# Two groups instead of one by seven block products in an attention and mixer kernel, with every engine's order written out

## The chip, the cores and the metric

The kernel runs on one core of one Trainium2 chip. The core has five engines with instruction queues of their own that run in order: TensorE (PE, matrix products into PSUM), VectorE (DVE), ScalarE (ACT), GpSimd (POOL) and SyncE (SP, which here only issues DMAs). Semaphores tie them together. The metric is the device time in microseconds (us), the median of several runs. Before the change it is 247.61 us (three runs, 247.29 to 248.21).

## The reference

```python
# linear attention, batch 8, heads 8, sequence 576, head size 64
phi(x) = np.where(x > 0, x, np.exp(x) - 1.0) + 1.0
kv  = einsum('bhsd,bhse->bhde', phi(k), v)      # per head
num = phi(q) @ kv;  den = phi(q) @ sum(phi(k)) + 1e-6
x   = num / den                              # to [8, 576, 512]
# mixer
h   = maximum(x.T @ w_tok1, 0) @ w_tok2      # along the sequence, 576 -> 256 -> 576
u   = x + h.T
h2  = maximum(u @ w_ch1, 0) @ w_ch2          # along channels, 512 -> 1536 -> 512
out = u + h2                                 # fp32
```

The kernel computes in bf16 with fp32 sums.

## The kernel before

The eight batches follow one another. A batch's 576 positions are four tiles of 128 and a tail of 64; the tails of two batches are handled together. For each batch the steps are:

- loads of q, k and v (576 KB each half) by SP into one buffer per tensor for batches 2 to 7 (`load`, L132);
- phi: an exponential on ACT (`phi_exp`, L151), add and max on DVE (`phi_add`, L157), a minimum on DVE (`phi_end`, L165); a cast of v (`vcast`, L176);
- `kv` (L191) on PE with copies on ACT (L197); phi(q) is transposed by a DMA (`qtr_dma`, L221); `nd_all` (L261) gives numerators and denominators on PE, and DVE divides (L270 to L289);
- `mm1` (L312) and `mm2` (L325), the token mixing, and the residual add on DVE (L337) that gives u; u is transposed by a DMA (`utr_dma`, L521) into uT, which the next step reads;
- the first channel mixing, `mm3` (L543): twelve chunks of 128 of the 1536 channels, each 4 matmuls of 512 columns, read by a Relu on ACT (L550) into cr;
- the second channel mixing by a seven-product block scheme (Strassen's, in Winograd's form): `row_sums` (L655) make sums of blocks of cr on DVE, `pair_product` (L852) makes seven products, `pair_copy` (L857, ACT) and `pair_end` (L861, DVE, and L863, POOL) put them together with u, and `pair_put` (L867) sends the batch out by POOL's queue.

In batches 2 to 6 four of the twelve chunks (4, 5, 10 and 11) do not go through `mm3` but also through seven block products (`mix_one`, L712). A group g takes chunks 2g and 2g+1 of the first half of the channels and the same chunks of the second half. Products 1 to 7 are 4 matmuls of 256 columns each. Their right sides are blocks of uT and four sums of such blocks (`u_sums`, L689, into tuc); their left sides are blocks of the weights and four sums of these (`group_sums`, L700, into swc), made once. Products 1, 6 and 5 are copied from PSUM by ACT (L720), product 4 is read by a Relu on ACT (L718), and products 2, 3 and 7 by a DVE operation that adds the copy and takes the Relu (`add_relu`, L531). Products 1, 6, 7 and 4 accumulate on one PSUM bank one after the other, with a read between them; 5 and 3 do so on another. Batch 7 does this for all three groups (`mix_first`, L740) and its second mixing without pairs (`product`, L768, `product_read`, L778).

The order of the work is the order of the calls, since the kernel is under a manual schedule. Each stage of batches 0 to 6 is a list `big` of PE's steps and a list `fill` of (position, step) that are put between them; batch 7 follows a string, `SEQUENCE`. A PSUM bank comes from a ring or from small tables beside each function. Output tiles come from eight slots that are taken in turn (`o_slots`), four a batch.

Of the kernel before, what the change touches and what calls it, by code (L numbers as in the profile page):

```python
# [15 lines left out]
EPS = 1e-6  # L16


@with_exitstack
def kernel(  # L20
# [43 lines left out]
    ring = {1: 0, 2: 0}  # L64

    def bank(at=None):
        if at is None:
            at, ring[1] = ring[1], (ring[1] + 1) % 4
        return psum[:, at]

    def banks(at=None):
        if at is None:
            at, ring[2] = 4 + ring[2], (ring[2] + 2) % 4
        return psum[:, at:at + 2]

    def two16():
        return banks().bitcast(BF16).rearrange("p a (t s) -> p a t s", s=128)
# [24 lines left out]
    uTj = [t.rearrange("p r j c -> p (r j c)").rearrange("p (j r c) -> p j r c", j=NDM, r=R) for t in uT]  # L102
    uTt = const("uTt", [128, 2, NDM, 128])
    cr = [const(f"cr{b}", [128, NCH, SM]) for b in range(2)]
    crt = const("crt", [128, NCH, 128])
    obuf = const("obuf", [128, 8, DM], FP32)
    swc = const("swc", [128, 4, 2, 256])
# [31 lines left out]

    live = {}  # L140
    o_at = [0]

    def o_slots(m):
        at = o_at[0] if o_at[0] + m <= 8 else 0
        o_at[0] = (at + m) % 8
        return obuf[:, at:at + m]

    def phi_exp(nm, n, j0, nj):
        f = raw[nm, rb(n)][:, j0:j0 + nj].rearrange("p j f -> p (j f)")
        e = work.tile([128, 2 * TD], BF16, name="e", tag="e", bufs=4)[:, :nj * TD]  # L150
        nc.scalar.activation(out=e, in_=f, func=AF.Exp)  # L151
        live["e", nm, n, j0] = e

    def phi_add(nm, n, j0, nj):
        f = raw[nm, rb(n)][:, j0:j0 + nj].rearrange("p j f -> p (j f)")
        y = work.tile([128, 2 * TD], BF16, name="y", tag="y")[:, :nj * TD]
        nc.vector.tensor_scalar(out=y, in0=f, scalar1=1.0, scalar2=1.0, op0=ALU.add, op1=ALU.max)  # L157
        for j in range(nj):
            live["y", j0 + j] = y[:, j * TD:]

    def phi_end(nm, n, j0, nj):
        c, i = divmod(j0, 2)
        dst = (kp if nm == "k" else qp)[:, c, :, i:i + nj]
        e, y = live["e", nm, n, j0], live["y", j0][:, :nj * TD]
        live["phi"] = nc.vector.tensor_tensor(  # L165
            out=dst.transpose([0, 2, 1, 3]), in0=e.rearrange("p (i t d) -> p i t d", i=nj, t=T),
            in1=y.rearrange("p (i t d) -> p i t d", i=nj, t=T), op=ALU.min)

    def phi(nm, n, c):
        phi_exp(nm, n, 2 * c, 2)  # L170
        phi_add(nm, n, 2 * c, 2)
        phi_end(nm, n, 2 * c, 2)

    def vcast(n, c, copy=nc.scalar.copy):
        js = slice(2 * c, 2 * c + 2)
        copy(out=vs[:, js, :, 0:D],  # L176
             in_=raw["v", rb(n)][:, js].rearrange("p j (t d) -> p j t d", t=T))

    def bank16():
        return bank().bitcast(BF16).rearrange("p (t s) -> p t s", s=128)  # L180
# [3 lines left out]
    def kv(n, cs):  # L184
        b = n % 2
        ps = banks(4 if n > 1 else None)[:, :, 0:2 * D1].rearrange(
            "p a (c e) -> p a c e", c=2)
        for c in cs:
            for t in range(T):
                for a, i in QUARTERS:  # L190
                    nc.tensor.matmul(out=ps[half[i], a, c], lhsT=kp[half[a], c, t, i],  # L191
                                     rhs=vs[half[a], 2 * c + i, t],
                                     start=(t == 0), stop=(t == T - 1))
        cs = slice(cs[0], cs[-1] + 1)
        for i in range(2):
            at = slice(i * D1, (i + 1) * D1)
            nc.scalar.copy(out=kvbd[b][half[i], cs, :, at].transpose([0, 2, 1, 3]),  # L197
                           in_=ps[half[i], :, cs])
# [6 lines left out]
    TS = [range(0, 5), range(5, T)]  # L205

    def qtr_put(n, c, ts, tp, put, dst=None):
        v_ = (qT[n % 2] if dst is None else dst)[:, 0:4 * TD].rearrange("p (a c t s) -> p a c t s", a=2, c=2, t=T)
        put(out=v_[:, :, c, ts[0]:ts[-1] + 1].transpose([0, 2, 1, 3]),
            in_=tp[:, 0:len(ts)].rearrange("p t (a s) -> p t a s", a=2))  # L210

    def qtr(n, c, put=nc.scalar.copy):
        tp = two16()
        for h, ts in enumerate(TS):
            qtr_mm(c, ts, tp[:, h])
        for h, ts in enumerate(TS):
            qtr_put(n, c, ts, tp[:, h], put)

    def qtr_dma(n, halves=range(2)):
        for a in halves:  # L220
            live["crossbar"] = nc.sync.dma_start_transpose(  # L221
                out=qT[n % 2][:, 2 * TD * a:2 * TD * (a + 1)].rearrange("p (f s) -> p f s", s=D),
                in_=qp[half[a]].rearrange("p c t i d -> p (c t i d)"))

    def nd_mm(n, c, rs):
        b = n % 2
        ps = banks()
        for s_, r in enumerate(rs):
# [5 lines left out]
        live["nd", c, rs[0]] = ps  # L234

    def nd_end(n, g, rs):
        b = n % 2
        m = len(rs)
        v_ = live["nd", g, rs[0]][:, 0:m, 0:HG * D1].rearrange("p r (h e) -> p r h e", h=HG)
# [9 lines left out]

    def nd_all(n):
        b = n % 2
        ps = [psum[:, 2 + 2 * m:4 + 2 * m] for m in range(3)]
# [10 lines left out]
        xv = x[b].rearrange("p r (c i a d) -> p i (r c) a d", c=2, i=2, a=2)  # L265
        v_ = [ps[m][:, :, 0:D1 * 7].rearrange("p i (k e) -> p i k e", k=7) for m in range(3)]
        dens = work.tile([128, 2, 2, 7], FP32, name="dens", tag="dens", bufs=1)
        last = work.tile([128, 2, 6], FP32, name="dens2", tag="dens2", bufs=1)
        both = psum[:, 2:6, 0:D1 * 7].rearrange("p b (k e) -> p b k e", k=7)
# [4 lines left out]
        def six(m, k0, rc0):  # L274
            den = (dens[:, m] if m < 2 else last)[:, :, k0:k0 + 6]
            nc.vector.tensor_tensor(  # L276
                out=xv[:, :, rc0:rc0 + 3],
                in0=v_[m][:, :, k0:k0 + 6, 0:D].rearrange("p i (q a) d -> p i q a d", a=2),
                in1=den.rearrange("p i (q a) -> p i q a", a=2)[
                    :, :, :, :, None].to_broadcast([128, 2, 3, 2, D]), op=ALU.mult)  # L280

        for m, at in enumerate((6, 0)):
            six(m, m, 4 * m)
            nc.vector.tensor_tensor(
                out=xv[:, :, 3, m], in0=v_[m][:, :, at, 0:D],
                in1=dens[:, m, :, at, None].to_broadcast([128, 2, D]), op=ALU.mult)
        nc.vector.tensor_scalar(out=last, in0=v_[2][:, :, 0:6, D], scalar1=EPS, scalar2=None,
                                op0=ALU.add)
        nc.vector.reciprocal(out=last, in_=last)  # L289
        six(2, 0, 7)  # L290

    def nd(n, g, rs):
        nd_mm(n, g, rs)
        nd_end(n, g, rs)
# [1016 lines left out]
```

## Time and profile before

| | |
|---|---|
| median of three runs | 247.61 us |
| span of the profiled execution | 246.4 us, 1.2 below the median |
| PE busy | 236.1 us (96%) |
| DVE busy | 198.8 us (81%) |
| ACT busy | 139.3 us (57%) |
| POOL busy | 76.9 us (31%) |
| DMA | 48.40 MB, mean 196 GB/s |
| L543, the chunks with 512 columns | 252 records, 60.2 us |
| L712, the products of the one group in five batches | 140 matmuls of 256 columns, 20.2 us |

Busy time is a union of an engine's instructions, with the parts in which a matmul drains while the next runs; so PE's 96% does not say by itself how full its stream is. A group's line gives the number of its instructions and, after the bar, busy time and mean length of one in ns, then the engine's idle time before them and what ended it. In a timeline each row is a start, a length, the engine, the line, and the tiles written and read.

### The profile page before, as it was taken

Reading aid. Unit: us, or ns where it says so; the run is one execution under the profiler, and the core shown is the slowest. Engines: PE = TensorE matmul, PEld = TensorE weight load, DVE = VectorE, ACT = ScalarE, POOL = GpSimd, SP = SyncE. Lnnn points to the kernel's source line nnn. Section 1 sums busy time; section 2 is a strip of 40 time slices with the busy share of each in tenths; the row PEclk is TensorE's granted clock in tenths of the full one; section 3 lists DMA queues with packets and bytes.
Section 4 is the critical chain, followed back from the end, with each engine's and each line's share of the span. In section 5 each row is a group of like instructions: output and inputs, shape, how many; then the busy total and the mean of one; then the engine's idle time right before and its main releaser. Section 6 shows DMA issues by size and latency. Waiting matters only on the chain.

```text
span 246.4 us, 6090 instructions
## 1 busy us (share of the span) xinstructions
PE 236.1 (96%) x2477; PEld 162.3 (66%) x2496; DVE 198.8 (81%) x349; ACT 139.3 (57%) x224; POOL 76.9 (31%) x88
## 2 busy tenths in 40 slices
PE   7789999999999899999999999999999999999993
PEld 3475455564868456865678556865676567888883
DVE  5955877889799998988894499979996779956973
ACT  4673881569774367736897167656852652175100
POOL 9670030296703600061004500071007700440360
PEclk9999999999999999999999999999999999999999
DMA  6999999999726796589979955459748702352055
GB/s 248 267 203 258 348 275 308 355 251 289 294 24 133 223 334 271 132 224 210 358 263 174 412 148 192 93 115 329 228 89 94 170 3 43 64 112 61 4 127 130
DMA packets 50444, 48.40 MB, mean 196 GB/s; under 512 B 30192, under 2 KB 36720, under 8 KB 50416
## 3 DMA queue, kind: packets, MB, share of 16 engines
q1 hardware_dynamic: 41984, 35.00, 48.2%
q0 software_dynamic: 7472, 12.22, 22.7%
q10 hardware_dynamic: 960, 0.79, 1.4%
q8 instruction: 19, 0.31, 0.5%
q14 instruction: 9, 0.07, 0.1%
HBM read 35.85 MB, written 9.44 MB: 184 GB/s over the span
## 4 chain that ended last, share of the span: by engine, by line
PE 84%; DVE 6%; DMA 5%; issue 3%; ACT 1%; SPq 0%; DVEq 0%
PE ps L543 22%; PE ps L852 18%; PE ps L712 6%; PE ps L312 6%; PE ps L583 5%; PE ps L740 4%; PE ps L768 4%; PE ps L325 4%; DMA q_raw<-in_q_dram 3%; PE ps L557 2%; PE ps L570 2%; DMA uT<-u 2%; PE ps L820 2%; PE ps L261 2%; PE ps L191 1%
## 5 line engine op out<-in xcount | busy, mean ns | idle before, releaser
L543 PE MATMUL ps<-uT,wc 128*128 128x512 bf16 x252 | 60.2, 379 | 0.8 <-DMA uT<-u 0.5
L550 ACT ACTIVATE cr<-ps 128x512 bf16<-128x512 f32 x59 | 34.7, 600 | 32.9 <-PE ps L543 32.7
L543 PEld LDWEIGHTS <-wc 128*128 128x128 bf16 x256 | 24.1, 98 | 25.1 <-DMA uT<-u 0.8
L863 POOL TENSOR_TENSOR obuf<-obuf,q_raw 128x512 f32<-128x512 f32 x6 | 8.1, 1344 | 93.3 <-DVE obuf L861 59.1
L852 PE MATMUL ps<-k_raw,v_raw 128*128 128x256 bf16 x216 | 24.9, 273 | 0.0
L852 PEld LDWEIGHTS <-v_raw 128*128 128x128 bf16 x216 | 21.0, 98 | 3.9 <-issue 0.4
L852 PEld LDWEIGHTS <-cr 128*128 128x128 bf16 x216 | 21.1, 98 | 3.7
L861 DVE TENSOR_TENSOR obuf<-ps,u 128x512 f32<-128x512 f32 x24 | 16.3, 685 | 8.1 <-PE ps L852 5.8
L151 ACT ACTIVATE e<-q_raw 128x1152 bf16<-128x1152 f32 x16 | 18.3, 1163 | 7.3 <-DVE x L244 5.5
L151 ACT ACTIVATE e<-k_raw 128x1152 bf16<-128x1152 f32 x16 | 18.2, 1165 | 2.7 <-DMA k_raw<-in_k_dram 2.7
L852 PE MATMUL ps<-wc,cr 128*128 128x256 bf16 x144 | 17.7, 273 | 0.0
L276 DVE TENSOR_TENSOR x<-ps,dens 128x768 bf16<-128x768 f32 x18 | 17.2, 953 | 0.4
L655 DVE TENSOR_TENSOR v_raw<-cr 128x768 bf16<-128x768 bf16 (+2 forms) x24 | 14.8, 617 | 2.1 <-ACT cr L718 2.1
L337 DVE TENSOR_TENSOR u<-ps,x 128x1024 bf16<-128x1024 f32 x12 | 14.6, 1217 | 0.4 <-PE ps L325 0.3
L176 ACT CAST vs<-v_raw 128x1152 bf16<-128x1152 f32 x12 | 13.5, 1161 | 0.0
L312 PE MATMUL ps<-x,w 128*128 128x512 bf16 x49 | 13.0, 379 | 0.3
L165 DVE TENSOR_TENSOR qp<-e,y 128x1152 bf16<-128x1152 bf16 x16 | 11.9, 753 | 1.6 <-ACT e L151 0.9
L165 DVE TENSOR_TENSOR kp<-e,y 128x1152 bf16<-128x1152 bf16 x16 | 12.7, 816 | 0.5 <-ACT e L151 0.4
L157 DVE TENSOR_SCALAR y<-k_raw 128x1152 bf16<-128x1152 f32 x16 | 11.7, 763 | 1.3 <-DMA k_raw<-in_k_dram 1.3
L157 DVE TENSOR_SCALAR y<-q_raw 128x1152 bf16<-128x1152 f32 x16 | 12.4, 793 | 0.4 <-DMA q_raw<-in_q_dram 0.4
L325 PE MATMUL ps<-ar,w2p 128*128 128x512 bf16 x44 | 11.8, 379 | 0.3
L583 PE MATMUL ps<-wc,cr 128*128 128x512 bf16 x47 | 11.9, 379 | 0.1
(182 smaller groups left out, 458.8 us busy)
## 6 DMA issues: line engine op xcount, KB each, us to landing
k_raw<-in_k_dram SPq DMA_DIRECT2D x16, 576.0 KB, 7.6
q_raw<-in_q_dram SPq DMA_DIRECT2D x16, 576.0 KB, 5.9
v_raw<-in_v_dram SPq DMA_DIRECT2D x14, 576.0 KB, 9.2
out_dram<-obuf POOLq DMA_DIRECT2D x12, 512.0 KB, 6.9
wc<-in_moe_w_ch_dram POOLq DMA_DIRECT2D x8, 384.0 KB, 9.8
out_dram<-obuf POOLq DMA_DIRECT2D x4, 256.0 KB, 6.0
out_dram<-obuf ACTq DMA_DIRECT2D x12, 64.0 KB, 2.2
out_dram<-obuf SPq DMA_DIRECT2D x12, 64.0 KB, 1.9
```

What stands on the lines that cost most here:

```text
L151: nc.scalar.activation(out=e, in_=f, func=AF.Exp)
L157: nc.vector.tensor_scalar(out=y, in0=f, scalar1=1.0, scalar2=1.0, op0=ALU.add, op1=ALU.max)
L165: live["phi"] = nc.vector.tensor_tensor(out=dst.transpose([0, 2, 1, 3]), in0=e.rearrange("p (i t d) -> p i t d", i=nj, t=T), in1=y.rearran ...
L276: nc.vector.tensor_tensor(out=xv[:, :, rc0:rc0 + 3], in0=v_[m][:, :, k0:k0 + 6, 0:D].rearrange("p i (q a) d -> p i q a d", a=2), in1=den.r ...
L312: nc.tensor.matmul(out=ps[:, mt], lhsT=w1t[:, b, ms] if r == R else w1[:, r, ms], rhs=x[b][:, r, :], start=(r == 0), stop=(r == R))
L325: nc.tensor.matmul(out=ps[:, i], lhsT=w2v(kt, r, b), rhs=ar[b][:, kt, :], start=(kt == 0), stop=(kt == NT - 1 and not add))
L543: nc.tensor.matmul(out=ps, lhsT=wc1[:, kj, 128 * mc:128 * mc + 128], rhs=uTj[b][:, kj] if n < 2 else uT[b][:, :, kj], start=(kj == 0), sto ...
L550: nc.scalar.activation(out=cr[b][:, mc, :], in_=ps, func=AF.Relu)
L583: nc.tensor.matmul(out=ps, lhsT=crt[:, kc, :] if t == 8 else cr[b][:, kc, 128 * r:128 * r + 128], rhs=wc2[:, kc, :], start=(kc == 0), stop ...
L655: return engine.tensor_tensor(out=s_[which - 1][:, ks], in0=x_, in1=y_, op=op)
L852: nc.tensor.matmul(out=live[tile_][:, j], lhsT=lhs[:, k_], rhs=rhs[:, k_], start=(first and j == 0 and k_ == 0), stop=(k_ == KH - 1), skip ...
L861: nc.vector.tensor_tensor(out=o, in0=live[tile_], in1=u[n % 2][:, d::2, HC[c]], op=ALU.add)
```

## The change

- Group 1 (chunks 2, 3, 8 and 9) of batches 2 to 6 goes through the seven block products as well. `mix_one` becomes `mix_mm` and `mix_read` with the group as an argument, swc holds the weight sums of both groups, and group 1's three copies lie in the spaces of the third and fourth row sums (`HOLD`).
- obuf has six output slots instead of eight; the batches 1 to 6 all use slots 0 to 3.
- Every step is split into a part for each engine, and each part has a name, such as `4x12` (batch 4, group 1, product 2 on PE) or `4y12` (its read). One string, `ORDER`, lists all names from batch 0 to 7, and the program is emitted in that order. The PSUM bank of each step is in a table, `BANK`, the buffers of the exponentials and of y in `EBUF` and `YBUF`, the output slots in `SLOT`. `GATE` names the four loads that wait for another transfer.
- In the program, matmuls of 512 columns go from 466 to 386 and those of 256 from 961 to 1101; DVE has 19 instructions more, 15 that add and take the Relu and 4 weight sums; ACT and POOL have as many as before, and so have the DMAs.

```diff
+NO = 6
+GSW = {2: 0, 1: 1}
+HOLD = {2: 'p0 p1 p2', 1: 's2 s3 s2'}
+GATE = {'1k0': ('wc1', 0), '2q0': ('wc2', 1), '4q0': ('u', 2, 1), '7q0': ('u', 5, 1)}
...
+BANK = {k_: int(v_) for k_, v_ in (e.split(":") for e in """2K:5 2n0:2 2n1:4 2n2:6 2f:2 2g0:5 2g1:2 2X2:7 2Z2:0 2Y2:2 2gt:6 3K:6 3n0:2 3n1:4 3n2:6 3f:3 3g0:2 3g1:4 3X2:1
...
+SLOT = {k_: int(v_) for k_, v_ in (e.split(":") for e in """0o0:0 0o1:2 1P:0 V0:4 2P:0 3P:0 V1:4 4P:0 5P:0 6P:0 7P0:4 7t:0 7P1:2""".split())}
...
+ORDER = """A2 A0 A1 A3 A4 A5 A6 A8 A9 A7 A10 A12 A13 A14 A11 A16 A17 A15 A19 A18 A21 A20 A22 A23 A24 A25 A26 A27 A28 A29
...
+2m7 5Lq1 2r1 W0 2s1 4kx0 4qb1 2x21 2x11 2s2 1o 3n1 2x22 2y21 2x25 2r7 2y22 2x26 2y25 2x15 2s3 2y11 2x12 2s4
+2y26 2x23 2y12 2r0 2x16 4qa0 4qx0 2x27 3f0 2y23 2y15 2y27 2y16 2p10 4qb0 3fr0 2x13 4v0 2w10 2x17 4qT0 2y13 3f1
...
-    ring = {1: 0, 2: 0}
-
-    def bank(at=None):
-        if at is None:
-            at, ring[1] = ring[1], (ring[1] + 1) % 4
-        return psum[:, at]
+    def bank(name):
+        return psum[:, BANK[name]]
...
-    obuf = const("obuf", [128, 8, DM], FP32)
-    swc = const("swc", [128, 4, 2, 256])
+    obuf = const("obuf", [128, NO, DM], FP32)
+    swc = const("swc", [128, len(GSW), 4, 2, 256])
...
-    def group_sums():
-        a11, a12, a21, a22 = [cblock(m, h)[:, :, 512:768] for m in range(2) for h in range(2)]
...
+    def group_sums(g, which):
+        s_ = swc[:, GSW[g]]
+        a11, a12, a21, a22 = [cblock(m, h)[:, :, 256 * g:256 * g + 256] for m in range(2) for h in range(2)]
...
+    def mix_read(n, g, i):
+        ps = mix_tile(n, g, i)
+        if n == B - 1:
+            c1, c6, c5 = hold[g]
+        else:
+            c1, c6, c5 = [hold_at[w[0]][int(w[1])] for w in HOLD[g].split()]
+        dst = lambda m, e: cr[n % 2][:, KH * m + 2 * g:KH * m + 2 * g + 2, HALF[e]]
+        if i == 4:
+            nc.scalar.activation(out=dst(1, 0), in_=ps, func=AF.Relu)
+        elif i in (1, 6, 5):
+            nc.scalar.copy(out={1: c1, 6: c6, 5: c5}[i], in_=ps)
+        else:
+            o, c = {2: (dst(0, 0), c1), 3: (dst(0, 1), c6), 7: (dst(1, 1), c5)}[i]
+            add_relu(o, ps, c)
...
+    for n in range(2, B):
+        for g in range(3) if n == B - 1 else GSW:
+            for i in range(1, 8):
+                put(f"{n}x{g}{i}", mix_mm, n, g, i)
+                put(f"{n}y{g}{i}", mix_read, n, g, i)
...
+    for name in ORDER.split():
+        tok[name]()
```

In the names, the first digit is the batch. `m` is a chunk of 512 columns and `r` its read, `x` and `y` a block product of the first mixing and its read, `s` a sum of blocks of uT, `G` a sum of weight blocks, `w` a row sum, `p` a product of the second mixing, `c`, `e`, `h` its copies, its adds on DVE and its adds on POOL, `o` the output DMAs, `n` the normalisation, `f` and `g` the token mixing, `K` the key-value product, `uT` and `qT` the transposing DMAs, `L` a load, and `T`, `U`, `V`, `W` a tail.

## The prediction

> **What bounds the kernel now.** I read the page's first part, then the chain, the waits of TensorE (PE), the timelines around the two places where PE stood still, and the busy time by stretch.
>
> ```profile
> PE 236.1 (96%) x2477; PEld 162.3 (66%) x2496; DVE 198.8 (81%) x349; ACT 139.3 (57%) x224; POOL 76.9 (31%) x88
> ...
> PE 84%; DVE 6%; DMA 5%; issue 3%; ACT 1%; SPq 0%; DVEq 0%
> ```
>
> PE is busy 96% of the span and 84% of the chain that ended last, so what is taken from PE's stream can show in the time. A busy PE need not be a full one, so next come starts. In the chain, stretches of one shape give the pace:
>
> ```profile
> 53.30 7.34 PE ps L543 x34
> ...
> 156.49 3.93 PE ps L852 x36
> ```
>
> A 512-column matmul takes 7.34/34 = 0.216 us from start to start, a 256-column one 3.93/36 = 0.109 us. Between 21 and 242 us nearly every pair of matmuls keeps this pace. Two gaps do not:
>
> ```profile
> 82.98 1.90 PE L543 MATMUL ps<-uT,wc 128*128 128x512 bf16 x8
> 85.50 0.80 PE L261 MATMUL ps<-kvbd,qT 64*128 64x65 bf16 x40 [0.62 <-DVE obuf L610]
> ...
> 187.64 1.47 PE L852 MATMUL ps<-q_raw,cr 128*128 128x256 bf16 x12
> 189.61 1.68 PE L543 MATMUL ps<-uT,wc 128*128 128x512 bf16 x7 [0.50 <-DMA uT<-u]
> ```
>
> Eight matmuls of 0.216 us from 82.98 on reach 84.71, and the next starts at 85.50: 0.79 us lost, for a bank that VectorE (DVE) had not read. Twelve of 0.109 from 187.64 on reach 188.95, and the next starts at 189.61: 0.66 us lost, for a transposing DMA. Together 1.4 us of stall; the rest is PE's own work.
>
> ```profile
> 63.00:84.00 21.00, 20.89 (x244) 15.29 (x244) 20.37 (x31) 12.08 (x17) 7.67 (x7) 1.00 0.51 138
> 84.00:109.20 25.20, 24.48 (x274) 16.88 (x274) 23.35 (x41) 16.55 (x25) 4.91 (x7) 1.00 0.78 241
> ...
> 139.20:164.40 25.20, 25.10 (x277) 17.15 (x278) 22.73 (x38) 16.47 (x25) 3.97 (x5) 1.00 0.59 170
> ```
>
> The columns are length, PE, PEld, DVE, ACT, POOL busy, then PE's granted clock (1.00 throughout). The reader is to see DVE's column: 20.4 of 21.0, 23.4 of 25.2 and 22.7 of 25.2 us. DVE is the second bound, and the change gives it work.
>
> **The PE term.** In batches 2 to 6 four chunks of the first channel mixing, each 4 matmuls of 512 columns, become seven products of 4 matmuls of 256. Per batch 16 x 0.216 = 3.46 us go, 28 x 0.109 = 3.05 us come: -0.40 us, over five batches -2.0 us. The other matmuls are the same in number and shape, only moved. All of it lies on PE's stream, so it counts in full if nothing else becomes late.
> [...] The rows above say 0.109 and 0.216, a half, and the measurement decides.
>
> **The ACT term: zero.** Four Relu reads (L550, 600 ns) become three copies (L720, 579 to 588 ns) and one Relu (L718, 591 ns) per batch. ACT is busy 16.5 of 25.2 us in the stretch above. What hides it is PE's stream; with that cover gone it would cost nothing more, being no longer.
>
> **The DVE term.**
>
> ```profile
> L531 DVE CUSTOM_DVE_ANT_0 cr<-ps,part 128x512 bf16<-128x512 f32 x6 | 4.1, 688 | 2.5 <-PE ps L740 1.6 <-ACT part L720 0.8
> L276 DVE TENSOR_TENSOR x<-ps,dens 128x768 bf16<-128x768 f32 x18 | 17.2, 953 | 0.4
> ```
>
> Per batch three add-and-Relu reads are new (L531, 0.69 us long, 0.61 apart back to back): +1.8 us. Once, four sums of weight blocks for the second group (L700, 0.42 us undisturbed): +1.4 to 1.7 us. Together +10.8 us on an engine that is busy 198.8. The batch from 139.2 goes from 22.7 to 24.5 us of DVE work while its PE work goes from 25.2 to 24.8; the one from 84.0 goes from 23.4 to 25.1, more than its PE work of 25.2 - 0.8 - 0.4 = 24.0, unless work moves to a neighbour. So the redrawn order decides. I added up DVE's and PE's new queues between the same marks, with durations of the batch from 139.2 (normalisation with L276 4.1 us a batch, phi 8 x 0.67, row sums 3.9, residual adds 2 x 1.14, output adds 4 x 0.61). From the normalisation products of batch 2 to those of batch 4 it has 42.0 us of DVE work against 44.2 of PE (95%), from 4 to 5 29.2 against 33.3 (88%), from 5 to 7 40.8 against 43.7 (93%). It fits everywhere, because batches 4 and 5 now start their first chunks before the last products of the batch in front, and some of phi and of the weight sums stands earlier. Following batches 2 and 3 read by read with PE at full pace, DVE is ready ahead of each consumer by little: 0.2 us for batch 2's last product of group 1, 0.3 for product 6 of its second mixing, 0.4 for product 3, 0.35 for batch 3's product 7 of group 2.
> Every new wait stands in such a chain: a product with its copy and the next product on the same bank. Behind a late DVE read stand the other DVE reads in its queue, and for them PE's next product. Each late read costs PE what exceeds its margin. From below: 0, since all margins are positive, and no gain beyond the removed gaps; from above, DVE's idle time of 2.5 us in the batch from 139.2 (25.2 - 22.7) stays as it is, which gives a batch of 24.5 + 2.5 = 27.0 us. I take +0.6 us over the five batches, nearest to the lower end, since the margins are positive in every stretch I followed and the tightest load is 95%.
>
> **The moved steps.** The gap at 84.71 goes: between the tail's last product and batch 3's normalisation, which needs its bank, now stand 2.1 us of other PE work for the tail's reader (L610 before). So does the one at 188.95: batch 6's last residual add is ready some 5.8 us of PE work ahead of its first consumer, and that transfer took 5.2 us at its longest (median 3.1 us). -1.4 us for both; what is late next is batch 7's first transfer, with about 4.6 us of PE work ahead of its consumer, between those two figures, bound 0 to +0.6 us, taken at 0 (the median). On SP the transposes now stand between loads, and only two loads still wait for a transpose; the tail's transpose of batch 3 stands behind three loads, where that transfer took 8.1 us in the median, with 9 us of PE work ahead of its reader: 0, and up to +2 if the loads are slower.
> POOL issues the same work. Its adds hold up DVE where DVE's operands are all in SBUF:
>
> ```profile
> 78.91 2.49 DVE L165 TENSOR_TENSOR kp<-e,y 128x1152 bf16<-128x1152 bf16 x2
> 81.32 1.27 DVE L861 TENSOR_TENSOR obuf<-ps,u 128x512 f32<-128x512 f32 x2
> 82.52 1.11 DVE L700 TENSOR_TENSOR swc<-wc 128x512 bf16<-128x512 bf16 x1
> ...
> 79.07 1.71 POOL L863 TENSOR_TENSOR obuf<-obuf,q_raw 128x512 f32<-128x512 f32 x1 [0.59 <-DVE obuf L861]
> 82.08 1.27 POOL L863 TENSOR_TENSOR obuf<-obuf,w 128x512 f32<-128x512 f32 x1 [1.29 <-DVE obuf L861]
> ```
>
> The two phi ends should take 1.42 us and took 2.49; the weight sum took 1.11 for 0.42. The PSUM read between them kept its 0.68. In the new order POOL's adds and its weight sums stand beside normalisation reads, which come from PSUM, so I count nothing; where an SBUF operation falls beside one, the price is up to 1.1 us of DVE.
> [...]
> Six output slots for eight: every batch now writes the same four. A batch's first output add comes 15 us of PE work or more after the DMA of the one before is issued, and that DMA lands in 6.9 us: hidden; with the cover gone, up to 7 us once.
> The prologue to 21 us and the 3.8 us behind the last matmul keep their instructions: 0.
>
> **Sum.** 246.4 - 2.0 - 1.4 + 0.6 = 243.6 us of span. The runs' median of 247.6 lies 1.2 above the profiled span, for what lies around it: 244.8 us.
>
> **Rivals.**
> A: DVE becomes the bound, slower. For it: 95% of load in the first two mixed batches, and in-order reads each of which waits for PE or ACT. Against: the margins above. Its place is batches 2 to 6; it decides from the point where DVE's idle time per batch exceeds 25.2 - 24.5 = 0.7 us. With half of today's 2.5 us the batch is 25.75, +0.55 x 5 = +2.8, less the removed gaps: 247.6 - 1.4 + 2.8 = 249.0. With all of it, +1.8 x 5: up to 255.
> B: the order hides nothing more than before: the stream gets shorter, but new small waits eat it (0.5 us a batch, one lost margin each, 2.5 in all): 247.6 - 2.0 - 1.4 + 2.5 = 246.7, no change.
> C: a transpose is late behind loads at one or two places: +2 to +4, 247 to 249.
> D: PE's stream gets no shorter: that needs 3.46 / 28 = 0.123 us for a 256-column matmul, and all such groups show 0.109; 246.8.
>
> **How the numbers follow.** Saturated stream 0.70 (243.2 to 246.3); B 0.12; A 0.12 (half of it below 250); C 0.06, half each side of 248.8. Low end: no new wait, and another 1 us of small gaps of 0.1 to 0.3 us gone too: 244.8 - 0.6 - 1.0 = 243.2. High end 249.2, A at half its idle time. The saturated case alone spans 243.2 to 246.3. A measurement here tells about 0.5% from no change, 1.2 us. Faster 0.71, same 0.14, slower 0.15.
>
> **What would show it.** Right: 80 matmuls of 512 columns fewer and 140 of 256 more at 0.216 and 0.109 us; DVE about 209 us busy, over 90% from 63 us on, PE's waits still under 2 us between 21 and 240. Wrong: PE waits for DVE's L531 counterparts or for banks, several times 0.3 us in each of batches 2 to 6 (A, B); PE waits for a transpose (C); DVE operations of over 1 us beside POOL's adds.

## The result

The changed kernel takes 248.70 us (median of 15 runs, 247.87 to 249.53), the kernel before 247.35 us (15 runs beside them): ratio 1.0043, 95% interval 1.0030 to 1.0056. Forecast were 244.8 us and a gain; it is a loss of 1.35 us, small (0.4%) but with an interval that leaves out no change. In short: PE's stream did get shorter, by half of what was forecast, and the last stores to DRAM came late by more than that.

The kernel before was profiled once more as a control: span 245.9 us, time 247.72. In the 15 runs of the changed kernel time minus span is 1.73 to 1.87 us, in the control 1.8. So the profile that the prediction was read from (span 246.4) belongs to a run of 248.2 us, one of the slower ones, and not to the median.

The profile after, its first part and its chain:

```profile
PE 235.1 (95%) x2538; PEld 168.5 (68%) x2556; DVE 204.1 (83%) x368; ACT 136.9 (56%) x224; POOL 78.7 (32%) x88
...
PE 88%; DVE 3%; DMA 3%; issue 2%; ACT 2%; DVEq 0%; SPq 0%; ACTq 0%
```

PE is busy 1.0 us less than in the first profile, DVE 5.3 us more; PE's share of the chain is 88% where it was 84%. These shares don't show the loss. I cut both traces at three marks: the start of the first channel-mixing matmul, the start of the last matmul, the end of DVE's last output add.

| us | control | changed | forecast of the change |
|---|---|---|---|
| up to the first channel-mixing matmul | 20.54 | 20.43 | 0 |
| from there to the last matmul | 221.35 | 219.87 (-1.48) | -2.8 |
| last matmul to the end of the last add | 0.74 | 0.73 | 0 |
| end of the last add to the end of the span | 3.32 | 5.53 (+2.21) | 0 |
| span | 245.9 | 246.6 | -2.8 |

PE wins half of what was forecast, and the stretch behind the last add eats more than that. One profile stands on each side. PE's stretch in the second row is 221.34 to 221.36 us in three of four profiles of the kernel before and 219.3 to 220.2 us in nine of ten of the changed kernel (runs with another store order or warm-up, told below, counted in), so that its gain is known to some 0.5 us. PE's timeline in the changed kernel has three places where a pair of rows does not close up:

```profile
33.09 1.03 PE L736 MATMUL ps<-wc,cr 128*128 128x512 bf16 x4
34.61 1.17 PE L309 MATMUL ps<-identity,qp 128*128 128x128 bf16 x18 [0.50 <-ACT cr L684]
...
141.58 1.05 PE L917 MATMUL ps<-uT,wc 128*128 128x256 bf16 x8
142.91 0.60 PE L917 MATMUL ps<-crt,swc 128*128 128x256 bf16 x4 [0.28 <-ACT q_raw L932]
...
162.99 1.47 PE L959 MATMUL ps<-wc,q_raw 128*128 128x256 bf16 x12
164.72 0.79 PE L376 MATMUL ps<-kvbd,qT 64*128 64x65 bf16 x40 [0.26 <-DMA qT<-qp]
```

Four matmuls of 0.216 us from 33.09 end their turn at 33.95, and the next starts at 34.61: 0.66 us, for ACT's read of a bank. Eight of 0.109 from 141.58 reach 142.45: 0.46 us, for a copy on ACT. Twelve from 162.99 reach 164.30: 0.42 us, for a transposing DMA. None of them is DVE's. The same stretches as in the prediction (84.0 and 139.2) show how full DVE is now:

```profile
84.00:109.20 25.20, 25.09 (x326) 18.50 (x321) 24.35 (x43) 16.04 (x25) 7.39 (x9) 1.00 0.75 218
...
139.20:164.40 25.20, 24.87 (x293) 18.47 (x292) 22.92 (x39) 15.29 (x24) 5.01 (x6) 1.00 0.71 180
```

24.35 of 25.2 us in the first, and PE's column beside it says 25.09: DVE is busy 97% of it, and the profile lists no wait of PE for DVE between 21 and 241 us.

The end of both kernels, in timelines of DVE, SP and ACT. The last batch's output goes out in 24 stores of 64 KB, one half of each quarter tile by SP and one by ACT. The control:

```profile
242.20 0.42 DVE L778 TENSOR_TENSOR obuf<-ps,u 128x256 f32<-128x256 f32 x1 [0.25 <-PE ps L768]
...
241.36 1.76 SPq L798 DMA_DIRECT2D out_dram<-obuf  x3
```

The last add ends at 242.62, and SP's last three issues are over at 243.1: the last stores go out when their adds end. The changed kernel:

```profile
240.61 0.42 DVE L1019 TENSOR_TENSOR obuf<-ps,ut 128x256 f32<-128x256 f32 x1 [0.23 <-PE ps L1012]
...
234.84 1.19 SPq L978 DMA_DIRECT2D out_dram<-obuf  x2
236.73 1.67 SPq L978 DMA_DIRECT2D out_dram<-obuf  x1
243.20 0.55 SPq L1024 DMA_DIRECT2D out_dram<-obuf  x1
...
236.42 1.99 ACTq L978 DMA_DIRECT2D out_dram<-obuf  x1
```

The last add ends at 241.03, 1.6 us sooner, but the last store is issued at 243.20, 2.2 us after it. Two things stand out. SP's first store goes out at 234.84, while ACT's goes out at 232.83. And one issue on each queue, both in progress at 237, takes 1.67 and 1.99 us instead of 0.55; both end at 238.40. From 236.45 to 238.02 one packet of 16 KB of program code, a code fetch, is under way; it is the last of 20:

```profile
q8 instruction: 20, 0.33, 0.5%
```

That queue carried 19 such fetches in the kernel before, the last of them at 230.5 us, before the first store at 232.8.

### The profile page after: what moved, and what is told of

It is laid out like the page before. It is cut to its first block, busy times and chain, and to the rows that moved or that the text cites. A ratio compares the mean times of both kernels' runs of the same rounds, so it can differ in the third digit from the quotient of the medians.

```text
span 246.6 us, 6211 instructions
## 1 busy us (share of the span) xinstructions
PE 235.1 (95%) x2538; PEld 168.5 (68%) x2556; DVE 204.1 (83%) x368; ACT 136.9 (56%) x224; POOL 78.7 (32%) x88
## 4 chain that ended last, share of the span: by engine, by line
PE 88%; DVE 3%; DMA 3%; issue 2%; ACT 2%; DVEq 0%; SPq 0%; ACTq 0%
PE ps L959 24%; PE ps L917 16%; PE ps L675 15%; PE ps L437 6%; PE ps L736 6%; PE ps L448 4%; PE ps L700 2%; PE ps L722 2%; PE ps L291 2%; PE ps L1012 2%; PE ps L376 2%; DMA k_raw<-in_k_dram 2%; DMA qT<-qp 1%; PE ps L309 1%; PE ps L616 1%
## 5 line engine op out<-in xcount | busy, mean ns | idle before, releaser
L675 PE MATMUL ps<-uT,wc 128*128 128x512 bf16 x171 | 40.9, 379 | 0.2
L684 ACT ACTIVATE cr<-ps 128x512 bf16<-128x512 f32 x39 | 22.4, 600 | 23.3 <-PE ps L675 18.1
L959 PE MATMUL ps<-k_raw,v_raw 128*128 128x256 bf16 x252 | 31.6, 273 | 0.0
L675 PEld LDWEIGHTS <-wc 128*128 128x128 bf16 x176 | 16.7, 98 | 16.7 <-issue 0.2
L959 PE MATMUL ps<-wc,cr 128*128 128x256 bf16 x168 | 21.6, 273 | 0.1
L917 PEld LDWEIGHTS <-swc 128*128 128x128 bf16 x160 | 15.6, 98 | 3.5 <-issue 0.5
L917 PEld LDWEIGHTS <-wc 128*128 128x128 bf16 x156 | 15.1, 98 | 4.1
L917 PE MATMUL ps<-crt,swc 128*128 128x256 bf16 x120 | 15.5, 272 | 0.3 <-ACT q_raw L932 0.3
L825 DVE TENSOR_TENSOR v_raw<-cr 128x512 bf16<-128x512 bf16 (+3 forms) x24 | 14.6, 618 | 0.0
L1058 POOL TENSOR_TENSOR obuf<-obuf,w 128x512 f32<-128x512 f32 x6 | 7.8, 1294 | 21.0 <-DVE obuf L1051 21.0
L437 PE MATMUL ps<-x,w 128*128 128x512 bf16 x50 | 13.9, 379 | 0.4
L917 PE MATMUL ps<-uT,wc 128*128 128x256 bf16 x104 | 14.1, 273 | 0.0
L264 ACT CAST vs<-v_raw 128x1152 bf16<-128x1152 f32 x12 | 13.9, 1162 | 0.0
```

Of the source, the lines that this page charges most:

```text
L437: nc.tensor.matmul(out=banks(f"{n}f")[:, mt], lhsT=w1t[:, b, ms] if r == R else w1[:, r, ms], rhs=x[b][:, r, :], start=(r == 0), stop=(r = ...
L675: nc.tensor.matmul(out=bank(f"{n}m{mc}"), lhsT=wc1[:, kj, 128 * mc:128 * mc + 128], rhs=uTj[b][:, kj] if n < 2 else uT[b][:, :, kj], start ...
L684: nc.scalar.activation(out=o, in_=ps, func=AF.Relu)
L825: return engine.tensor_tensor(out=s_[which - 1][:, ks], in0=x_, in1=y_, op=op)
L917: nc.tensor.matmul(out=ps[:, j], lhsT=lhs[:, k_, 128 * j:128 * (j + 1)], rhs=rhs[:, :, k_], start=(first and j == 0 and k_ == 0), stop=(k_ ...
L959: nc.tensor.matmul(out=ps, lhsT=lhs[:, k_], rhs=rhs[:, k_], start=(first and not skip and k_ == 0), stop=(k_ == KH - 1), skip_group_check= ...
```

## The experiments

**The control** (`before_again`, no edit):

> The kernel before, unchanged, as a control. In the runs of the changed kernel the time lies 1.73 to 1.87 us above the span. If the same holds for the kernel before, its median of 247.35 us belongs to a span near 245.55 us, and the profiled execution (246.4 us) was one of its slower ones (248.21). Expected: ratio 1.000, spans of 245.3 to 246.4, time minus span 1.8 us. The rival (my prediction's own reading): the span is 246.4 and the time lies 1.2 us above it. No 16 KB code fetch after 232 us, no store issue longer than 0.8 us.

Measured 247.62 us, ratio 1.0006 (0.9995 to 1.0018); the profiled execution has a span of 245.9 us at a time of 247.72. The base of the prediction is settled as the expectation has it: the time is 1.8 us more than the span.

Two theories on the tail. Q: the order in the store queues. In the kernel before, each read issues its stores itself (`product_read`, `tail_read`). In the changed one reads (`7R`, `7tr`) and stores (`7D`, `7td`) are separate names (`7D300` is the store behind product 3 of pair 0; the last digit is 0 on SP and 1 on ACT), and on SP the store `7D300`, ready at 234.8, stands ahead of `7D700` and `7D210`, ready since 232.8 and 232.5. F: the code fetch. PE's program became longer by 120 instructions (60 matmuls, each with its weight load), and a 20th fetch falls among the stores. The rival to both, R: two queues at 0.64 us a store are simply full.

**The stores in order of readiness** (`after_stores`), and the kernel before with the changed kernel's queue order (`before_stores`):

```diff
-7R40 7R30 7t6 7D401 7ts3 7tr2 7D300 7R61 7D211 7p51 7tr6 7D700 7R20 7D301 7t5 7td20 7R51 7D201 7p71 7D210 7tr5
...
+7R21 7D210 7D211 7R70 7D700 7D701 7p30 7ts4 7tb2 7p40 7p20 7R40 7D400 7D401 7R30 7D300 7D301 7t6 7ts3 7tr2 7td20
```

```diff
+    waiting = ["D30 D70 t2 D21 D20 D40 D71 t7 t3 D31 D41 t4".split(),
+               "D70 D40 D21 D30 D20 t2 D71 t7 t3 D31 D41 t4".split()]
...
+            while waiting[e] and waiting[e][0] in ready[e]:
+                ready[e].pop(waiting[e].pop(0))()
```

> The changed kernel with the last batch's 24 small stores issued in the order in which their adds end (only SP's and ACT's queues change). Theory Q (order in the queue): in the changed kernel SP's first store waits for an add that ends at 234.8 us while two others have been ready since 232.5 and 232.8 us behind it; so SP starts 2.0 us late and, at 0.64 us for a store, never catches up: the last store goes out 2.2 us after the last add. In order of readiness SP starts at 232.5 us, even with the code fetch the last store goes out some 0.6 us after the last add, and the time falls by about 1.6 us, from 248.7 to 247.1 us. Rival R (rate): both queues need 7.7 us for their 12 stores and the fetch's stall decides; then ACT's queue, whose order matters less, still ends late and the time falls by at most 0.5 us, to 248.2 us.

> The kernel before, its 24 last stores put into SP's and ACT's queues in the order of the changed kernel (on SP first the store after product 3 of pair 0), nothing else changed. Theory Q (order in the queue): in the profile of before that product's add ends at 237.84 us and SP's 12 stores at 0.64 us each then end with one issued at 244.9 instead of 243.1; on ACT the second store waits for an add that ends at 239.14, and the last goes out at 245.5 instead of 243.3. The time rises by 1.8 to 2.2 us, from 247.6 to 249.4 to 249.8 us. Rival F (the code fetch alone makes the stores late): this kernel has no fetch among its stores, so the time stays within 0.4 us of 247.6.

Measured: 246.72 us for the first, ratio to the kernel before 0.9972 (0.9957 to 0.9987); 250.36 us for the second, 1.0121 (1.0103 to 1.0140), more than forecast. The timelines, first of the ordered one:

```profile
240.65 0.42 DVE L1018 TENSOR_TENSOR obuf<-ps,ut 128x256 f32<-128x256 f32 x1 [0.23 <-PE ps L1011]
...
232.57 3.08 SPq L977 DMA_DIRECT2D out_dram<-obuf  x4
...
241.74 0.55 ACTq L1023 DMA_DIRECT2D out_dram<-obuf  x1
```

and of the kernel before with the other order:

```profile
242.14 0.42 DVE L787 TENSOR_TENSOR obuf<-ps,u 128x256 f32<-128x256 f32 x1 [0.25 <-PE ps L777]
...
237.37 1.19 SPq L807 DMA_DIRECT2D out_dram<-obuf  x2
...
245.48 0.61 ACTq L845 DMA_DIRECT2D out_dram<-obuf  x1
```

The ordered kernel starts its stores at 232.5 and has a backlog of 0.7 us at the end. The kernel before, whose last add ends when the control's does (242.57), starts its stores on SP at 237.37 instead of 232.39 and issues the last one 2.9 us after the add. Q is shown in both directions; R falls, since the same 24 stores at the same pace keep up when they stand in the right order. A second run of the ordered kernel (`stores_again`, on another chip) was less good:

> The changed kernel with its stores in order of readiness once more, unchanged, on the same chip as the one above: 246.7 us again (246.4 to 247.1), ratio to the kernel before 0.997.

Measured 247.19 us, 0.9985 (0.9972 to 0.9999), just above the range that was expected. So the order alone makes the changed kernel 0.15 to 0.3% faster than the kernel before. Its profile has two store issues of 2.02 and 1.72 us beside the fetch, which leads to F.

**Moving the fetch.** Five ways of changing the number of PE instructions ahead of the stores; the first takes warm-up matmuls away, the others put more and shorter ones in (lines abridged; the runs' names stand behind #):

```diff
-lambda: warm(0, 4),  lambda: warm(1, 2, 256),  lambda: warm(2, 1, 256),
+lambda: warm(0, 3),  lambda: None,  lambda: None,                  # after_no_fetch
...
-    warm(4)
+    warm(3)
+    pad(72)                                                        # before_pad, 2 columns each
...
+lambda: (warm(0, 4), pad(40)),                                    # after_fetch_early
+lambda: (pad(10), num_first(0, 0, R)),
+lambda: (pad(10), num_first(1, 0, 2)),
+lambda: (pad(10), utr_first(1, dve)),
...
+lambda: warm(0, 32, 64),                                           # after_warm64, stores_warm64
...
+lambda: warm16(0, 62),                                             # after_warm16, stores_warm16; 44 in stores_warm44
```

> The changed kernel with 16 PE instructions fewer (one of the four long warm-up matmuls in the prologue and the three short ones are left out; they fill idle time and feed nothing). [...] With 5113 instructions there are 19 fetches as in the kernel before, no store issue over 0.8 us, the last store goes out 1.1 to 1.3 us earlier, and the time falls from 248.7 to about 247.5 us. Rival R (rate): the two queues are simply full, with too many stores under way; then an issue of 1.5 to 2 us still stands near 236.4 us and the time stays at 248.7 us (within 0.4).

> The kernel before with 140 PE instructions more: 72 matmuls of two columns in the prologue's idle time in place of one long warm-up matmul. [...] If only the new order of the changed kernel makes its stores late (Q or R), the fetch costs at most 0.3 us here, since the stores of this kernel have no backlog: 247.4 to 247.7 us.

> The changed kernel with 140 PE instructions more in the prologue (70 matmuls of two columns where PE waits; all warm-up matmuls are kept). Theory F: the 20th code fetch comes 140 instructions sooner, near 229 us, before the first store; no store issue takes over 0.8 us any more, the last store goes out some 1.1 us sooner, and the time is 247.5 to 247.8 us (248.7 without the change). The queue order keeps its cost: the last store still goes out 0.8 to 1.2 us after the last add. If the fetch is harmless (the queues are full anyway), the time stays at 248.7; if the added matmuls hold up the prologue, PE's first channel-mixing matmul starts later than 20.6 us by what they cost, which then has to be taken off.

> The changed kernel with its four long warm-up matmuls (512 columns, float32) cut into 32 of 64 columns: the same columns, so that PE stays as busy, but some 112 PE instructions more. Theory F once more, this time without idle PE in the prologue: the 20th code fetch comes near 230.5 us, before the first store; no store issue over 0.8 us, the last store goes out 0.9 to 1.2 us after the last add instead of 2.2, and the time is 247.5 to 247.8 us instead of 248.7. If the clock is granted in full (1.0 up to the last matmul), the prologue is as before and the whole difference is the fetch's. If the fetch is harmless: 248.7 us.

> The same with the stores in order of readiness (246.72 us). There the fetch held one store issue for 1.46 us, of which 0.67 us of delay was left at the end (last add 241.07, last store issued 241.74). With the fetch out of the way the last store goes out 0.1 to 0.3 us after the last add: 246.2 to 246.4 us. If the fetch is harmless: 246.7 us.

> The changed kernel with the four long warm-up matmuls (float32, 512 columns, 6.8 us) replaced by 62 of 256 columns in bfloat16 (62 x 0.109 = 6.8 us): PE stays as busy and loads its weights at the usual pace, and has 108 instructions more. The code fetch comes near 231 us, before the first store. Theory F: tail from the last add to the end of the span 4.5 us as in the two other runs with an early fetch (5.5 in the changed kernel), prologue as before, time 247.6 us. If the fetch is harmless: 248.7 us.

> The same with the stores in order of readiness (246.72 us): tail 3.3 us (3.7 with the fetch among the stores), prologue as before, time 246.3 us, 0.4 per cent under the kernel before. If the fetch costs nothing there: 246.7 us.

> The last kernel (stores in order of readiness, warm-up in bfloat16) with 44 warm-up matmuls for 62. The 62 took 8.75 to 9.24 us instead of 6.8, since the first 16 to 21 of them started 0.213 us apart and not 0.109, and the prologue was 1.5 to 2.1 us longer for it. 44 need some 18 x 0.213 + 26 x 0.109 = 6.7 us and are done before phi(q) at 8.3 us; the fetch comes near 231.6 us, still ahead of the first store at 232.5. Tail 3.3 us, prologue as in the changed kernel: 246.3 us (0.4 below the kernel with the stores in order alone, 1.1 below the kernel before). If the slow start of the bfloat16 matmuls lasts past 18 of them, up to 247.3 us.

As times all of these missed (F's forecast for `before_pad` was 248.4 to 248.7 us). The first seven paid in the prologue (251.05, 249.21, 251.76, 255.88, 255.17, 248.81, 247.85 us; what happened there is told at the end), and the last is told below. The first did not even lose its fetch: with 16 instructions fewer there were still 20; how many instructions one packet holds no run shows. Their tails, which no prologue touches, say it all the same:

| end of the last add to the end of the span, us | stores in the changed order | in order of readiness |
|---|---|---|
| fetch among the stores | 5.53, 5.40 | 3.70, 3.77, 4.15, 4.74 |
| no fetch among them | 4.46, 4.47, 4.46 | 3.31, 3.31, 3.31, 3.32 |

(Upper row: the changed kernel, `after_no_fetch`; `after_stores`, `stores_waits`, `stores_best2`, `stores_again`. Lower row: `after_fetch_early`, `after_warm64`, `after_warm16`; `stores_warm64`, `stores_best3`, `stores_warm16`, `stores_warm44`. In the last of them the fetch, at 234.17 us, stands beside the first two stores, behind which the queues pause.) In the seven of the lower row no store issue takes over 0.9 us; each of the six of the upper row has one or two of 1.2 to 2.0. In `before_pad` the fetch came at 238.36, where the queues pause between stores (238.65 to 239.87), and its tail is 3.33 us: a fetch alone need not cost. So, taken in this order, the 2.2 us are the queue order's 1.15 (4.46 - 3.31) and the fetch's 1.07 (5.53 - 4.46); in order and without fetch the tail is the control's 3.32. The two are not fixed prices. With the stores in order the fetch cost 0.4 to 1.4 us in four runs, and in the kernel before the other order alone, with no fetch among the stores, made the tail 6.01 us, 2.7 more than the control's. The end of `stores_warm16`:

```profile
242.42 0.42 DVE L1018 TENSOR_TENSOR obuf<-ps,ut 128x256 f32<-128x256 f32 x1 [0.23 <-PE ps L1011]
...
243.10 0.55 ACTq L1023 DMA_DIRECT2D out_dram<-obuf  x1
```

The last add ends at 242.85, the last store follows 0.25 us later. How a code packet holds up the issuing queues is not shown; that both held issues of the changed kernel end 0.4 us after the packet is. The version with 44 warm-up matmuls, the only one with a nearly normal prologue (0.5 us longer), takes 247.12 us, 0.9984 (0.9971 to 0.9997); in its profiled run PE also stood still for 1.05 us from 116.96, where the first tail's chunks wait for their transposing DMA. 246.3 was forecast: a miss.

**The core of the change undone** (`stores_chunks2`), on the ordered kernel:

(Batch 4 alone is shown, abridged.)

```diff
-... 4x11 ... 4y11 ... 4x12 ... 4x16 ... 4y16 4x15 ... 4y12 4x17 ... 4y15 ... 4y17 4x13 ... 4y13 ... 4x14 ... 4y14
+... 4m2 ... 4r2 ... 4m3 ... 4m8 ... 4r8 4m9 ... 4r3 ... 4r9
```

> The core of the change undone once more, with the chunks and their Relu reads so early that every row sum finds its rows: in the kernel with the stores in order of readiness (246.72 us) groups 2, 3, 8, 9 of batches 2 to 6 by four chunks in the places of the products 1, 2, 6 and 5, the other three products and the four weight sums left out. Theory P: 80 matmuls of 512 columns for 140 of 256 give PE 2.0 us more, and no new wait on PE was caused by DVE's new reads: the last matmul starts 2.0 us later and the time is 248.7 us. If ACT, which now has four Relu reads for three copies and one Relu, gets late as in the first undone version (four new waits of 0.4 to 0.9 us for ACT's reads), up to 250 us. If the new DVE reads had cost PE waits (A, B), under 247.7 us.

Measured 250.41 us, 3.7 above the ordered kernel's first run. From the first channel-mixing matmul to the last it takes 224.32 us against 219.70: +4.6, of which 2.0 are the matmuls by their spacing; most of the rest are waits, here the longest:

```profile
PE ps L373 <- DMA qT<-qp: 0.9, 1, 0.9
PE ps L914 <- ACT ar L438: 0.8, 1, 0.8
PE ps L306 <- ACT cr L681: 0.5, 1, 0.5
```

DVE is busy 175.1 us between 20.5 and 240 instead of 188.6, and PE waits more, not less. So less work on DVE won PE nothing here. An earlier version (`stores_chunks`), with the chunks' reads later:

> The kernel with the stores in order of readiness (246.72 us), and the core of the change undone: groups 2, 3, 8, 9 of batches 2 to 6 by four chunks of 512 columns again, in the places of four of the seven products, with the Relu on ACT; the four weight sums on DVE are left out; everything else as in the new order. Theory P (the PE term of the prediction): PE gets 16 x 0.216 - 28 x 0.109 = 0.40 us more a batch, 2.0 us in all, and nothing else was bound by DVE: 248.7 us. Rival A/B (the new reads cost PE waits that eat the gain): with 1.8 us of DVE work less a batch PE loses less elsewhere, and the time rises by under 1 us: 246.7 to 247.7 us.

In it (252.02 us) some row sums stand ahead of a chunk's read and take older rows; it had four new waits for ACT's Relu reads. In both, other reads and waits changed along with the products, so neither is a clean price of the core.

**PE's new waits** (`stores_waits`, then `stores_best2`):

```diff
-1Q0:6 ... 1Q1:4 1K:4
+1Q0:4 ... 1Q1:6 1K:6                        # both
...
-4y21 6v0 4x26 3hW 5nd 4m7      -6n 4eY 4hW 5m0 6nd
+4y21 6v0 4m7 4x26 3hW 5nd      +5m0 6n 4eY 4hW 6nd          # stores_waits
...
-1Q01 1Q10 1Qc01 1Q11 1Qc10 0q2 1v1          -4w40 4c1 4p50 6qb0
+1Q01 0q2 1Q10 1Qc01 1Q11 1Qc10 1v1          +6qb0 4w40 4c1 4p50   # stores_best2
```

> The kernel with the stores in order of readiness (246.72 us), and three of PE's new waits taken away: batch 1's two transposes of phi(q) swap their PSUM banks (the wait of 0.66 us at 33.9 us for ACT's read of the bank), batch 4's chunk 7 goes ahead of product 6 of its second group (0.44 us at 142.5 for ACT's copy), batch 5's chunk 0 goes ahead of batch 6's normalisation products (0.37 us at 164.3 for the transposing DMA). If these waits lie on PE's stream one after the other, 1.4 us go: 245.3 us. Rival: PE stands still a little later instead (the order is tight, and each has a next constraint): at most 0.5 us go, 246.2 us or more.

> The kernel with the stores in order of readiness (246.72 us), two of PE's waits attacked in another way than before: batch 1's transposes of phi(q) swap their banks and batch 0's output chunk 2 (four matmuls of 512 columns, 0.86 us) stands between them, so that neither the bank's reader (0.66 us at 33.9) nor phi(q)'s second half (0.47 us at 35.3, which took its place in the earlier try) is waited for; and phi(q) of batch 6 ends ahead of one row sum of 0.95 us on DVE, so that its transposing DMAs start 0.9 us sooner (0.37 us at 164.3). If both are plain waits: 1.0 us go, 245.7 us. Rival (the order is tight, DVE's chain of the normalisation is next): under 0.3 us go, 246.5 us or more.

Measured 247.75 and 247.37 us: misses, and the rivals hold. In the first, PE's two longest waits are

```profile
PE ps L674 <- DVE x L401: 0.6, 1, 0.6
PE ps L916 <- DVE x L401: 0.5, 1, 0.5
```

the normalisation's division on DVE, one from 142.97 in place of the copy (chunk 7's bank is one that the division still reads) and one from 168.15 in place of the DMA; two more of 0.3 us are for the second half of phi(q) and for a load of weights. In the second the transposing DMA is no longer waited for, but the key-value product at 36.1 us waits 0.59 us for a copy of phi(q) on DVE. With the early fetch the last edit alone was run once more:

> The same, and phi(q) of batch 6 ends ahead of one row sum of 0.95 us on DVE, as in the earlier try, where PE's wait for the transposing DMA at 164.3 us (0.37 us) was gone; the banks in batch 1 stay as they are. If that wait was plain: 0.35 us less than the kernel without it, 245.9 us. If the row sum's lateness takes its place: no difference.

Its time, 255.52 us, holds the same long prologue as `stores_warm64`; PE's stretch is 219.90 us in both, so nothing was won. Where a wait was taken away, others came in its place.

**One store for two** (`stores_merged`; the last batch's eight pairs of halves, the tail's stay in two):

```diff
-[nc.sync, nc.scalar][e].dma_start(out=outv[n, :, 2 * (2 * j + d) + e, HC[c]], in_=o[half[e], d, HC[c]])
+if e == (i + j) % 2:
+    [nc.sync, nc.scalar][e].dma_start(
+        out=outv[n, :, 2 * (2 * j + d):2 * (2 * j + d) + 2, HC[c]].rearrange("p e c -> e p c"),
+        in_=o[:, d, HC[c]])
```

> The kernel with the stores in order of readiness (246.72 us), the two halves of each last store put into one DMA of 128 rows, by turns on SP and on ACT: 12 issues for 24. Theory R' (the tail's end is set by the number of issues, 0.64 us each on both queues): no queue has a backlog any more, even beside the code fetch, the last store goes out at the last add, 0.3 to 0.7 us sooner: 246.1 to 246.4 us. Rival: an issue costs by its rows (128 take about 1.1 us), or one DMA of 128 KB lands later than two of 64 KB: no gain, 246.7 to 247.3 us.

Measured 261.86 us: a miss. Issues became 16, most of 0.5 to 0.7 us, so twice the rows did not make an issue twice as long; but three issues held their queues up, two of them on SP, in these pairs:

```profile
235.97 5.65 SPq L978 DMA_DIRECT2D out_dram<-obuf  x2
242.48 5.94 SPq L1025 DMA_DIRECT2D out_dram<-obuf  x2
```

In each of these pairs one issue took 4 us (as one did on ACT), and the DMAs moved 48 GB/s in long stretches, where the small stores move some 200.

## Why the prediction was wrong

- **The step that failed** is "The prologue to 21 us and the 3.8 us behind the last matmul keep their instructions: 0." The instructions stayed, their order on SP's and ACT's queues did not, and the last code fetch came at 236.45 us instead of 230.5. Together the end became +2.21 us longer where 0 was put: 1.15 for the queue order, 1.07 for the fetch, by the table above. The prediction asked of moved steps which queues they pass and did so for the transposes; for the last stores it did not, though the diff listed them as names of their own.
- **The PE term, -2.0 us, was right**: 512-column matmuls still start 0.216 us apart, 256-column ones 0.109, and 80 fewer and 140 more were run. Rival D falls. The prediction rightly went by the rows.
- **The moved stalls, -1.4 us, did go, but one of them was not tied to its place.** The wait at 84.71 is gone (0.79 us); the control has it too, from 84.87, there put down to a read on ACT and not on DVE. The one at 188.95 is not in the control, whose PE runs on:

```profile
187.82 1.47 PE L852 MATMUL ps<-q_raw,cr 128*128 128x256 bf16 x12
189.13 1.89 PE L543 MATMUL ps<-uT,wc 128*128 128x512 bf16 x8
```

  Twelve of 0.109 from 187.82 end at 189.13. Instead the control waits at batch 1's key-value products for a load of weights, which the first profile does not; first that profile's rows, then the control's:

```profile
36.14 0.82 PE L191 MATMUL ps<-vs,kp 64*64 64x65 bf16 x72
36.90 1.04 PE L583 MATMUL ps<-wc,cr 128*128 128x512 bf16 x3
...
35.91 1.00 PE L191 MATMUL ps<-vs,kp 64*64 64x65 bf16 x72
37.11 1.02 PE L583 MATMUL ps<-wc,cr 128*128 128x512 bf16 x4 [0.20 <-DMA wc<-in_moe_w_ch_dram]
```

  The same products take 0.76 us in one and 1.20 in the other. From the first channel-mixing matmul to the last both have the same length, 221.36 and 221.35 us. The changed kernel has neither wait (0.85 us for these products). A wait for a DMA in one profile is one draw; whether the one wait keeps the other away is not shown.
- **The new waits, +0.6 us, were mis-sized, and in the wrong place.** -1.48 measured, with -2.0 for the matmuls and -0.8 and -0.4 for the control's two waits, leaves +1.7: 0.66 at 33.9, 0.46 at 142.5, 0.42 at 164.3 and small ones. Forecast were DVE's reads in batches 2 to 4; found were ACT's bank read in batch 1's transposes, where the order was redrawn too and the prediction had not followed it, one copy on ACT, and one transposing DMA (rival C's kind, a fifth of its price at most). This is the second term that failed, and it took PE's gain from 2.8 to 1.5 us.
- **The DVE term and rivals A and B**: DVE has 5.3 us more busy time than in the first profile (10.8 forecast, some 209 us). The 15 new reads are there, at 0.69 us each, but more of DVE's operations overlap: their lengths add up to 9.1 us more, and the time in which any of them runs grows by 5.3. No wait that the profile lists for PE between 21 and 241 us is for DVE. A falls. B's 2.5 us of small waits come near the 1.7 found, by chance: they are for ACT and a DMA in three places, not five lost margins of DVE's reads. Its 246.7 us is not the time of the changed kernel, whose further 2 us were lost at the end, which no rival named.
- **The base** was the median, so that a slow profiled execution did no harm to it; but its "1.2 us for what lies around" is 1.8.

The measured 1.35 us between the medians is more than the 0.62 between the two profiled spans; the changed kernel's profile lies 0.3 us below its median and the control's 0.1 above its own, which was in turn 0.27 above the median that the changed kernel was first compared with. The store stall, 1.2 to 2.0 us long from run to run, fits the wider spread of the kernels that have it, but was not measured in the unprofiled runs.

## What to carry to other kernels

Follow a redrawn order to the last DMA: SP and ACT issued the stores in the order of the program, and one that was ready late held up all behind it (the last was issued 2.2 us after the last add here and 2.9 in `before_stores`, 0.7 with the stores in order of readiness); at the end of a kernel nothing hides that. When a gain on the bounding engine does not arrive, measure the stretch from its last instruction to the end of the span first. Changes of the instruction count moved code fetches here (the 19th from 230.5 us to 220.9, and a 20th came at 236.45), and a forecast gain that rests on one DMA wait in one profile should be looked for in a second profile, together with the length of the whole stretch.

## What the runs showed of the hardware

- A code fetch that PE does not notice can still cost: in the six kernels of the table's upper row its 16 KB packet took 1.05 to 1.64 us among the stores, and a store issue beside it took 1.2 to 2.0 us instead of 0.55. PE's matmuls keep their pace beside it: in the changed kernel groups of six with 256 columns start at 236.48, 237.13, 237.79 and 238.44 us, 0.109 us a matmul, while the packet is under way to 238.02.
- PE's clock in the prologue. The kernel before and the changed kernel were granted 1.00 over their first 21 us. With 16 warm-up instructions fewer (`after_no_fetch`) it was 0.50 from 9.40 to 19.60 us, with 72 two-column matmuls in place of one long one (`before_pad`) from 8.45 to 11.80, with 70 of them in the gaps (`after_fetch_early`) from 16.40 to 23.20. The number after POOL's is the granted clock; first the run without the warm-ups from 9.4 us on, then the one with 70:

```profile
9.40:19.60 10.20, 9.00 (x147) 7.60 (x148) 5.85 (x11) 6.02 (x20) 5.92 (x9) 0.50 1.30 202
```

```profile
16.40:23.20 6.80, 5.95 (x29) 4.24 (x30) 1.48 (x3) 1.63 (x5) 1.89 (x3) 0.50 1.27 234
```

  What set the clock down, and why in the runs with more matmuls too, is not shown.
- In float32 a weight load took 0.33 us (329 ns in `after_warm64`; in bfloat16 98 ns in the changed kernel). Cut into 64 columns the warm-ups took longer: 64 records took 13.9 us, where the 8 of 512 columns took 5.9. That the weight loads set this pace is the author's reading. The first 17 to 26 of the bfloat16 warm-ups, in `after_warm16`, `stores_warm16` and `stores_warm44`, started 0.213 us apart and not 0.109, at a granted clock that the profile gives as 1.00 (means of the three profiled runs 0.994, 0.998 and 1.000); why is open.
- The merged store, with its two halves outermost, moved 48 GB/s in the long stretches, and the DMA engines were busy for one to two tenths of the time there; with 64 rows outermost the same bytes moved at some 200 GB/s, at seven to nine tenths (`before_again`). What makes the difference is not shown.
